# Two more pairs of token tiles with 15 block products for the channel mixer's first product, in a new order of the whole queue

## The chip, the core and the metric

The kernel runs on one core of a Trainium2 chip. The metric is device microseconds from the start to the end of one execution, and of several executions the median counts. The core has a matrix engine (PE, with its weight loads shown apart as PEld), three engines for elementwise work (DVE for vectors, ACT for activations and copies, POOL), and a queue (SP) that issues DMAs. Each engine works through its own list of instructions in program order; semaphores make one engine wait for another. Only PE writes to PSUM, from where DVE and ACT fetch the results.

## What is computed

A delta rule attention (4 batch elements, 8 heads, 768 tokens, head size 48) is followed by an MLP mixer over tokens and channels. All is in float32.

```python
for t in range(S):                      # the recurrence, for each element and head
    y[t]  = q[t] @ state
    v_old = k_n[t] @ state              # k_n: k divided by its norm
    state = state + beta[t] * outer(k_n[t], v[t] - v_old)
x = y with the heads side by side       # (4, 768, 384)
u = x + (relu(x^T @ w_tok1) @ w_tok2)^T # token mixer, 768 -> 256 -> 768
out = u + relu(u @ w_ch1) @ w_ch2       # channel mixer, 384 -> 1536 -> 384
```

## The kernel before, in words

**The recurrence** is chunked: 64 tokens a step, 12 steps an element, 48 steps in all (`recur`, job r0 to r47). Two steps make a unit of 128 tokens; there are 24 units, six an element. A unit is loaded (`load_kq`, job k), prepared (`prep`, p: norms, transposes, scaled masks), its Gram products are taken (`grams`, c and d, L440 on PE and L443 on DVE), a triangular matrix is inverted for a round of up to four units at once (`invert`, i: pairs of dependent DVE instructions L661 and L666; parts are turned by way of DRAM, L608 and L633), the halves are joined (`join`, j, L734 to L767), and v is scaled (`load_v`, v).

A step t of the recurrence goes back and forth between the engines: PE multiplies keys with the state (p_k, L790), DVE subtracts v (rest, L797), PE reads (p_y L810 and p_w L814), ACT copies (w_t, L820), PE makes the new state (p_s, L828) and the outputs (p_y, L829), DVE updates the state (s_t, L837). The next step's L790 needs that state. Element 0 has steps 0 to 11, element 1 steps 12 to 23, element 2 steps 24 to 35, element 3 steps 36 to 47.

**The mixer** of an element (`mixer`, jobs m0 to m3) can begin when its six units are written. The token mixer is L986 and L999. The channel mixer goes over three pairs of token tiles (256 tokens): transposes (L1009, copied on ACT, L1013), the first product with w_ch1, and the second product with w_ch2, which is done with 7 block products in place of 8 (L1088, whose results DVE adds to xb, L1017; the sums it needs are L1040, in `halves_of`).

For the first product there are two ways. The direct one takes 36 products of 128 x 128 with 256 columns (L1066), and ACT rectifies six results of 512 columns (L1075). In blocks of 128 tokens, 128 features and 512 channels this is 2 x 3 x 3 = 18 block products. The other way (`wide_fast`) takes 15 block products, which are 60 products of 128 x 128 with 128 columns (L958). It needs 11 sums of operands, 128 columns each (`forms`, L927 on DVE), and of its results 6 are copied by ACT (L967), 10 are added by DVE from PSUM (L970), and 6 are rectified by ACT (L974). Three PSUM buffers (tag mlp) are shared by all of the mixer.

The second way needs sums of blocks of w_ch1, too. They are made once, by job s (`sum_weights`, 16 sums, L899 and L897, on DVE), partly in place of blocks of w_ch1 that are not needed any more, partly in `lent`, the storage in which units 2, 3, 6, 7, 10 and 11 hold keys and queries. So the sums must come after the preparation of unit 11 (p11) and, where they overwrite blocks, after the direct products that read these. Before the change, all three pairs of element 0 go the direct way (`FAST = 1`) and the nine pairs of elements 1 to 3 the other.

**The order** in which all of this is emitted is one string of words, each a job's name and the number of pieces of it (a piece ends at each `yield`). Nothing else orders the work: each engine's list follows from it. It is written out in the kernel as text. Loading and rounding of weights are jobs w0 to w33 (L271 to L284; for w_ch2 L299 makes sums of blocks on DVE); x, z and Y are dummy products which keep PE busy (L225, L235).

Of the kernel before, what the change touches and what calls it, by code (L numbers as in the profile page):

```python
# [23 lines left out]
def kernel(  # L24
# [106 lines left out]
    NL = 2  # L131
# [64 lines left out]
    FAST = 1  # L196
# [145 lines left out]
    ranked = set()  # L342
    spread = set()
# [28 lines left out]
    def load_kq(u):  # L372
        b, c = divmod(u, NCH)
        kst = kst_of[slot(u)]
        if u >= TU:
            yield from load_rows(u, 0, k)
            assert last_in(u) in ranked
            yield from stacked(kst, k, u)
            yield from load_rows(u, 1, q)
            return  # L380
        for pad, src in ((kpad, k), (qpad, q)):
# [4 lines left out]
            )  # L386
            yield
            if src is k and u >= RU:
                yield from stacked(kst, k, u)

        heads = kpad[slot(u)].rearrange("t (p par) d -> t p par d", par=2)
        for cc in range(2 if u < RU else 0):
            for par in range(2):
                nc.scalar.copy(kst[PAR[par ^ cc], :, cc], heads[PAR[cc], :, par, 0:D])
                yield
# [57 lines left out]
    def prep(u):  # L453
# [7 lines left out]

        ksq = work.tile([128, NB, D], FP32, name="ksq", bufs=1)
# [20 lines left out]
        if u < TU:  # L483
            p_t = ps_turn([128, NP, 2, C], "p_t")
            for p in range(NP):
                nc.tensor.transpose(p_t[:, p], kp[:, 2 * p : 2 * p + 2], ident)
            turned.add((True, u))
# [14 lines left out]
        if u < TU:  # L502
            p_t = ps_turn([128, NP, 2, C], "p_t")
            for p in range(NP):
                nc.tensor.transpose(p_t[:, p], qp[:, 2 * p : 2 * p + 2], ident)
            turned.add((False, u))
# [220 lines left out]
    def join(u):  # L727
# [5 lines left out]
        assert done.issuperset([(u, 0), (u, 2)])  # L733
# [12 lines left out]
        for nb in range(NB):  # L746
            for r, r2 in halves:
                nc.tensor.matmul(p_z[r2, nb], wt[r, nb, HB:C], t11[r, nb])  # L748
                if before:
                    w = gm_of(before)[:, :, TC]  # L750
                    nc.tensor.matmul(p_x[r, nb], zst[r2, nb], w[r2, nb, HB:C])
        yield
        for r, r2 in halves:
# [11 lines left out]
        for nb in range(NB):  # L765
            for r, r2 in halves:
                nc.tensor.matmul(p_x[r, nb], zst[r2, nb], wt[r2, nb, HB:C])  # L767
        yield
# [96 lines left out]
    def sum_weights():  # L865
# [5 lines left out]

        a = {(j, k): (j, k) for j in range(3) for k in range(NCB)}
# [106 lines left out]
    def mixer(b):  # L979
# [42 lines left out]
        def turn_pair(c):  # L1022
# [4 lines left out]
            if b < FAST:  # L1027
# [5 lines left out]
        for c in range(0, NCH, 2):  # L1033
# [21 lines left out]
            if b >= FAST:  # L1055
# [4 lines left out]
            else:  # L1060
                for m in range(NM):
                    p_c = ps_mlp([128, 2, 2 * U], "p_c")
                    for k in range(2):
# [7 lines left out]
                        if (b, c) == (FAST - 1, NCH - 2):  # L1071
# [10 lines left out]
            turns = (*range(2, NM), 0, 1) if b >= FAST else range(NM)  # L1082
# [98 lines left out]
    r9*4 w4 i2*2 p10 i2*2 v5 i2 v5 w19 m0 r9 k10 j5 p10 i2 p10 v5 i2*2 w15 w4 v5*2  # L1181
    w4 r9*2 i2 m0 v7 k11 j5 i2 k11*2 r9 v7 j5 p10 i2 r10 v7 i2 w15*2 i2 k12 r10*3
    w15 r10 r9 m0 j5 r10*3 i2*3 r10 p10 d10 c10*3 w25 i2 c10 d10*2 w19 k12 w4 k11
    r11*3 k12*2 w19 k12 i2 r11 r10 m0 r11 i2 r11*2 d10 Y i2*3 r11 w12 r11 i2*2
    k12*3 Y w19 w21 v6 i2 v6 i2*2 m0 i2 k12 i2*2 k12*2 w12 v6 i2*2 Y v6*2 m0*2 v7
    p12*2 m0*2 c10 m0 p11*2 f6 w21 p11 f6*2 m0*2 w12*2 f7*2 m0 f7 w21 p10 m0 p11*2
    d10 w21 m0 p12 m0 j6*2 f6 p11 j6 f8*2 w25 m0 f7 f8 w23 f8 p11 j7*3 w25 p12 m0
    w25*2 r12*2 v7 r12*3 j8*2 w31 r12 t10 w23*2 t10 j8 f9*2 m0 w23 r12 r13 w23 w32
    f9 k12 r13*2 t10*2 r13 f9 p12 p11 w31*3 r12 w30 k13 p11*2 k13 m0 r13*2 d11 k13
    d11 c11*2 r13 w32*3 r13*2 d11 w30 r13 w20*2 c11 k13*2 c11*2 w30*2 r14*2 k13 d11  # L1190
    k13 d11 r14*3 p12*2 w29 m0*4 w20*2 v8 r14 k13 d12 r14 c12 d12 c12 d12 p13 c12
    d12*2 k13*2 r14 p13*2 r14*2 m0 k13*2 v8*2 r15 w23 c12*2 w25 r15*4 p12 p13*2 v8
    w33 t11 j9 m0*2 w31 r15 p13*2 t11 t12 k14*2 m0 k14 m0*2 w31 r15 m0 r15 p13
    r15*2 c13*2 w31 k14*2 d13 c13 t11 d13 c13 d13 r16 d13 r16 c13 k14 d13 w33*2 v8
    w33 w27 k14 w27 t12*3 w33 k14 t13 r16*3 w33 m0*2 j9 w27 m0*2 t11 w25 j9 r16
    t13*2 s w29 t13 w23 j9 r16*2 i3 p14 r16 w33 p14 m0 j9 v10*2 r17*2 k14 r17*2 v10
    r17 p14 v10 p14 v9 k14 p14 k15*2 i3 p14 m0*2 i3 m0 i3*3 r16 m0 i3*2 m0*2 k15
# [81 lines left out]
```

## Time and profile before

| | |
|---|---|
| median of 3 runs | 639.69 us (639.24 to 639.78) |
| profiled execution | 638.03 us |
| its span, first to last instruction | 636.3 us |
| busy PE, PEld | 606.3, 529.0 us |
| busy DVE, ACT, POOL | 447.3, 259.5, 108.7 us |
| mean granted clock of TensorE | 0.981 |
| DMA | 50.27 MB, mean 79 GB/s |

The times in the profile are of one execution. A group of instructions is one line of the kernel, with its engine, what it writes and reads, its count, its busy time and the mean length of one instruction, and then the idle time of the engine just before it and who ended it. A float32 product is two rows of PE in the trace, apart from the transposes, which are one. The ends of matmul rows are modelled, so that PE can show as busy while it waits for a short time; their starts are measured.

### The profile page before, as it was taken

What the parts mean: (1) busy time and instruction counts of PE and PEld (TensorE: products, weight loads), DVE (VectorE), ACT (ScalarE), POOL (GpSimd) and SP (SyncE); (2) the same over time, 40 slices, a digit from 0 to 9 for tenths busy, and PEclk for the clock granted to TensorE, in tenths of its full rate; (3) what the DMA queues carried; (4) which work ended last, traced back from release to release, by engine and by line L of the source; (5) the groups of instructions that cost most, each with busy time, mean ns of one, the idle gap of its engine ahead of it and who ended that gap; (6) DMA issues with size and microseconds to landing.
All of it is one profiled execution on the core that took longest, in us unless ns stands there. A gap on an engine that the chain in (4) does not pass through costs nothing.

```text
span 636.3 us, 21488 instructions
## 1 busy us (share of the span) xinstructions
PE 606.3 (95%) x9132; PEld 529.0 (83%) x9132; DVE 447.3 (70%) x1132; ACT 259.5 (41%) x631; POOL 108.7 (17%) x146
## 2 busy tenths in 40 slices
PE   8488798899999999999999999999999999999997
PEld 5367676667898988958999999769999987999997
DVE  4987876966899568988969987785627253373643
ACT  7758886447422242125623333135244230223240
POOL 2348364235301113021110010101010000000000
PEclk9878997899999999999999999999999999999999
DMA  9787568646442444354444033202020000000000
GB/s 201 131 145 170 138 133 206 151 111 155 104 111 60 92 110 92 81 131 79 92 103 101 13 94 49 66 10 38 2 54 2 27 2 0 26 1 26 1 26 26
DMA packets 135776, 50.27 MB, mean 79 GB/s; under 512 B 114656, under 2 KB 130144, under 8 KB 135680
## 3 DMA queue, kind: packets, MB, share of 16 engines
q1 hardware_dynamic: 135680, 48.89, 34.5%
q8 instruction: 72, 1.18, 0.8%
q14 instruction: 24, 0.20, 0.1%
HBM read 39.42 MB, written 9.44 MB: 77 GB/s over the span
## 4 chain that ended last, share of the span: by engine, by line
PE 81%; DVE 7%; ACT 5%; DMA 3%; issue 2%; SPq 1%; POOL 0%; DVEq 0%; ACTq 0%; POOLq 0%
PE p_o L1088 26%; PE p_r L958 19%; PE p_c L1066 7%; PE p L986 5%; PE p_h L999 5%; PE p_k L790 3%; PE p_s L828 3%; PE p_g L440 3%; PE p_y L810 3%; DMA d<-in_moe_w_ch_dram 1%; PE p_z L748 1%; PE p_ut L1009 1%; PE p_w L814 1%; DVE sub L661 1%; PE p_y L829 1%
## 5 line engine op out<-in xcount | busy, mean ns | idle before, releaser
L1088 PE MATMUL p_o<-wc,r 128*128 128x192 f32 x720 | 125.8, 329 | 0.6 <-ACT u_t L1013 0.6
L1088 PEld LDWEIGHTS p_o<-wc,r 128*128 128x128 f32 x720 | 116.7, 190 | 2.7 <-ACT u_t L1013 1.1
L970 DVE TENSOR_TENSOR r<-r,p_r 128x512 f32<-128x512 f32 x90 | 59.7, 684 | 39.9 <-PE p_r L958 38.8
L1017 DVE TENSOR_TENSOR xb<-xb,p_o 128x192 f32<-128x192 f32 x84 | 29.3, 350 | 59.5 <-PE p_o L1088 59.3
L967 ACT COPY r<-p_r 128x512 f32<-128x512 f32 x54 | 31.5, 584 | 91.4 <-PE p_r L958 89.8
L666 DVE TENSOR_TENSOR x<-x,sub 128x84 f32<-128x84 f32 (+24 forms) x178 | 59.6, 335 | 6.1
L661 DVE TENSOR_TENSOR sub<-x 128x84 f32<-128x84 f32 (+24 forms) x178 | 58.4, 328 | 7.1 <-DMA x<-n_dram 2.8
L1066 PE MATMUL p_c<-u_t,wc 128*128 128x256 f32 x216 | 51.2, 387 | 0.2 <-ACT u_t L1013 0.2
L1088 PE MATMUL p_o<-wc,s 128*128 128x192 f32 x288 | 50.5, 329 | 0.3 <-DVE xb L1017 0.3
L414 POOL TENSOR_TENSOR v_st<-v_st,nrm 128x384 f32<-128x384 f32 x24 | 20.6, 859 | 174.6 <-DMA v_st<-in_v_dram 140.7
L1088 PEld LDWEIGHTS p_o<-wc,s 128*128 128x128 f32 x288 | 46.8, 190 | 1.2 <-DVE xb L1017 0.6
L820 ACT COPY w_t<-p_w 128x192 f32<-128x192 f32 x48 | 15.3, 319 | 73.2 <-PE p_w L814 72.5
L1066 PEld LDWEIGHTS p_c<-u_t,wc 128*128 128x128 f32 x216 | 39.6, 190 | 5.9 <-ACT u_t L1013 0.4
L974 ACT ACTIVATE r<-r 128x512 f32<-128x512 f32 x54 | 33.8, 630 | 25.6 <-DVE r L970 25.3
L440 PE MATMUL p_g<-kq 48*64 48x128 f32 (+1 forms) x704 | 38.3, 290 | 3.3 <-ACT kq L509 3.3
L497 POOL TENSOR_TENSOR mb<-mask_c,cs 128x512 f32<-128x512 f32 x20 | 21.0, 1050 | 114.1 <-DVE gm L443 45.1
L842 ACT ACTIVATE xb<-p_y 64x192 f32<-64x192 f32 x96 | 31.1, 324 | 21.3 <-PE p_y L829 10.5
L958 PE MATMUL p_r<-u_t,wc 128*128 128x128 f32 x288 | 38.5, 277 | 0.0
L958 PE MATMUL p_r<-t_d,wc 128*128 128x128 f32 x288 | 37.2, 280 | 0.0
L443 DVE TENSOR_TENSOR gm<-p_g,mb 128x512 f32<-128x512 f32 x44 | 29.4, 683 | 10.0 <-PE p_g L440 7.2
L986 PE MATMUL p<-xb,w 128*128 128x384 f32 x96 | 35.6, 513 | 0.0
L958 PEld LDWEIGHTS p_r<-u_t,wc 128*128 128x128 f32 x288 | 35.3, 192 | 0.3
(177 smaller groups left out, 1200.1 us busy)
## 6 DMA issues: line engine op xcount, KB each, us to landing
d<-in_moe_w_ch_dram SPq DMA_DIRECT2D x24, 384.0 KB, 3.9
v_st<-in_v_dram SPq DMA_DIRECT2D x96, 48.0 KB, 2.5
out_dram<-xb SPq DMA_DIRECT2D x23, 192.0 KB, 1.9
kst<-in_k_dram SPq DMA_DIRECT2D x64, 48.0 KB, 3.2
n_dram<-gm SPq DMA_DIRECT2D x72, 32.0 KB, 2.4
pads<-in_k_dram SPq DMA_DIRECT2D x24, 96.0 KB, 2.4
pads<-in_q_dram SPq DMA_DIRECT2D x24, 96.0 KB, 2.5
gm<-w_dram SPq DMA_DIRECT2D x72, 32.0 KB, 2.1
```

Of the source, the lines that this page charges most:

```text
L440: nc.tensor.matmul(p_g[PAR[i ^ cc], p], kqt[f, p, cc, 0], kqt[f, p, cc])
L661: nc.vector.tensor_tensor(out=tmp, in0=y[:, :, 0:s, s : s + 1].to_broadcast([n, k, s, w]), in1=y[:, :, s : s + 1, s + 1 : m].to_broadcast( ...
L666: nc.vector.tensor_tensor(out=y[:, :, 0:s, s + 1 : m], in0=y[:, :, 0:s, s + 1 : m], in1=tmp, op=ALU.add,)
L842: nc.scalar.mul(y[:, :, D * i : D * i + D], p_y[PAR[1 - i]], 1.0 if c else -1.0)
L958: nc.tensor.matmul(p[:, i], pieces[i // width][:, at : at + 128], f[f"u{n}"], start=first and i == 0, stop=True, skip_group_check=True,)
L967: nc.scalar.copy(o, p)
L970: nc.vector.tensor_tensor(out=o, in0=o, in1=p, op=ALU.add if sign > 0 else ALU.subtract)
L974: nc.scalar.activation(o, o, ACTF.Relu)
L986: nc.tensor.matmul(p_1[dh], piece_of(w1, c, 0)[:, dh * 128 : (dh + 1) * 128], xb[:, c], start=(c == 0), stop=(c == NCH - 1),)
L999: nc.tensor.matmul(p_h, piece_of(w2, j, c * 128)[:, c * 128 : (c + 1) * 128], r1[j], start=(j == 0), stop=(j == NDH - 1),)
L1066: nc.tensor.matmul(p_c[:, k], piece_of(wc1, cb, f * 128)[:, f * 128 : (f + 1) * 128], u_t[:, cb], start=(cb == 0), stop=(cb == NCB - 1),)
L1088: nc.tensor.matmul(p, a[:, m], wc2[:, m, j], start=(start and i == 0), stop=(i == NM - 1), skip_group_check=True,)
```

## The change

Pairs two and three of element 0 (tiles 2 and 3, and 4 and 5) go the way with 15 block products; only the first pair stays direct. `FAST` is now the place (element, tile) from which on the other way holds. The weight sums so have to come between the first and the second pair of element 0. The string of the order is new from step 9 on, up to about step 36; before and after that the jobs come as they did. The rest of the diff are assertions, which build nothing (`keys_in`, `pads_in`, `held` and a loop in `sum_weights` check that an order reads nothing too early).

```diff
-    FAST = 1
+    FAST = (0, 2)
...
+        for u in range(NL, WIDE):
+            assert slot(u) < NL or u in ranked and turned.issuperset([(True, u), (False, u)])
...
-            if b < FAST:
+            if (b, c) < FAST:
                 return u_t, None
...
-            if b >= FAST:
+            if (b, c) >= FAST:
                 for ms in wide_fast(t_c, r2):
...
-                        if (b, c) == (FAST - 1, NCH - 2):
+                        if (b, c + 2) == FAST:
                             used.add(f)
...
-            turns = (*range(2, NM), 0, 1) if b >= FAST else range(NM)
+            turns = (*range(2, NM), 0, 1) if (b, c) >= FAST else range(NM)
...
-    r9*4 w4 i2*2 p10 i2*2 v5 i2 v5 w19 m0 r9 k10 j5 p10 i2 p10 v5 i2*2 w15 w4 v5*2
-    w4 r9*2 i2 m0 v7 k11 j5 i2 k11*2 r9 v7 j5 p10 i2 r10 v7 i2 w15*2 i2 k12 r10*3
+    r9*4 w4 Y r9 p10 w29 i2 w4*2 v5*4 w15 k11 i2*7 r9 i2 w15*2 i2 m0*2 x r9 j5
+    p10*2 r9*2 r10*2 k12 r10*2 v5 m0 w15 w4 i2 j5*2 i2*2 j5 r10 i2 k10 p10 i2 p10
...
-    f9 k12 r13*2 t10*2 r13 f9 p12 p11 w31*3 r12 w30 k13 p11*2 k13 m0 r13*2 d11 k13
-    d11 c11*2 r13 w32*3 r13*2 d11 w30 r13 w20*2 c11 k13*2 c11*2 w30*2 r14*2 k13 d11
+    w31 p11 w32 w31*3 p11 r13 p11 c11 k12 r13 p12 r13*2 s*4 r13 s*2 t10*3 d11 t10
+    w32*2 c11*3 s w30*4 v8*2 s c11 d11*2 w20 r14*2 d11*2 w32 p12*2 r14*3 k13*5 j9
...
```

In the changed kernel the 16 pieces of job s stand in the string between steps 13 and 16; before, twelve stood between steps 16 and 24 and four at step 28.

More of the change, by code (lines that the diff above doesn't have):

```diff
@@ L342 @@
     ranked = set()
+    keys_in = set()
+    pads_in = set()
+    held = {"t11": None, "zst": None}
     spread = set()
@@ L377, in load_kq @@
             assert last_in(u) in ranked
-            yield from stacked(kst, k, u)
+            for n, _ in enumerate(stacked(kst, k, u)):
+                if n == 3:
+                    keys_in.add(u)
+                yield
             yield from load_rows(u, 1, q)
@@ L751, in join @@
                     nc.tensor.matmul(p_x[r, nb], zst[r2, nb], w[r2, nb, HB:C])
+        assert held["zst"] == before
+        held.update(t11=None, zst=None)
         yield
+        assert held["zst"] is None
+        held["zst"] = u
         for r, r2 in halves:
```

124 lines of the change are left out of this document (65 added, 59 removed).

## Prediction

> **What bounds the kernel now.** I read the page first (busy shares, the 40 slices, the chain that ended last), then the chain in order of time, then the granted clock in short windows, and then the busy times of one stretch after another. The stretches are cut at steps of the recurrence, because the change moves everything else around these steps.
>
> ```profile
> span 636.3 us, 21488 instructions
> PE 606.3 (95%) x9132; PEld 529.0 (83%) x9132; DVE 447.3 (70%) x1132; ACT 259.5 (41%) x631; POOL 108.7 (17%) x146
> PE   8488798899999999999999999999999999999997
> DVE  4987876966899568988969987785627253373643
> PEclk9878997899999999999999999999999999999999
> ```
>
> (The last three rows are of the page's second part.) The reader is to see that PE is at 9 in nearly every slice from the ninth on, and that DVE is at 8 or 9 in many slices of the first half and only at 2 to 6 in the last third. So work taken from PE is worth its full time only where DVE can follow, and the change gives DVE work in just the half where it is nearly full.
>
> ```profile
> PE 81%; DVE 7%; ACT 5%; DMA 3%; issue 2%; SPq 1%; POOL 0%; DVEq 0%; ACTq 0%; POOLq 0%
> ```
>
> The chain confirms it: 81% of it is PE.
>
> The next rows give starts of single steps, from the timeline. "Update t" is L837 of step t (DVE), "rest t" is L797 (DVE), "read t" is the first L814 of step t (PE).
>
> ```profile
> 102.98 1.09 PE L790 MATMUL p_k<-s_t,kq 48*64 48x48 f32 x16 [0.46 <-DVE s_t L837]
> 153.07 0.35 DVE L837 TENSOR_TENSOR s_t<-s_t,p_s 128x192 f32<-128x192 f32 x1
> 214.87 0.32 DVE L797 TENSOR_TENSOR rest<-p_k,v_st 128x192 f32<-128x192 f32 x1
> 217.18 0.25 PE L814 MATMUL p_w<-rest,gm 64*64 64x48 f32 x1
> 260.38 0.43 PE L814 MATMUL p_w<-v_st,gm 64*64 64x48 f32 x8
> 402.52 0.55 PE L814 MATMUL p_w<-v_st,gm 64*64 64x48 f32 x12
> ```
>
> They are the beginning of step 9, update 13, rest 19, read 19, read 24 and read 36. Busy times of the stretches between them follow. Columns: length, then PE, PEld, DVE, ACT and POOL busy, granted clock, DMA share, GB/s.
>
> ```profile
> 103.00:153.10 50.10, 47.42 (x764) 33.73 (x766) 37.47 (x103) 25.68 (x66) 15.05 (x18) 0.93 0.63 150
> 153.10:214.90 61.80, 61.79 (x875) 55.00 (x868) 55.58 (x146) 20.20 (x52) 12.76 (x16) 1.00 0.42 98
> 214.90:217.20 2.30, 2.30 (x19) 2.08 (x17) 1.75 (x5) 0.00 (x0) 0.73 (x1) 1.00 0.50 93
> 217.20:260.40 43.20, 43.15 (x835) 37.43 (x834) 30.40 (x65) 15.35 (x41) 8.86 (x11) 1.00 0.50 106
> 260.40:402.50 142.10, 141.70 (x2203) 127.67 (x2202) 118.82 (x305) 50.89 (x122) 17.09 (x25) 1.00 0.35 79
> 402.50:636.30 233.80, 229.90 (x2557) 208.69 (x2556) 124.91 (x313) 68.05 (x142) 4.74 (x8) 1.00 0.07 19
> ```
>
> From update 13 to read 36 PE has no idle time to speak of. From update 13 to rest 19, though, DVE too is busy for 55.58 of 61.8 us: two engines are near their limits there at once.
>
> **The change, on PE.** Each of two pairs loses 36 products of 256 columns and gets 60 of 128. A product is two matmul rows in the trace. Undisturbed runs of each kind stand in the chain:
>
> ```profile
> 194.00 7.97 PE p_c L1066 x36
> 535.76 10.72 PE p_o L1088 x66
> 576.76 13.67 PE p_r L958 x120
> ```
>
> 72 rows of L1066 are 2 x 7.97 = 15.94 us; 120 rows of L958 are 13.67. A pair saves 2.27 us, both 4.5. All else on PE only moves, apart from a few dummy matmuls. The two kernels' instruction lists give the move in counts: from update 13 to read 19 the changed kernel has 33 products of L1066 less, 24 of L1088 less and one set of L958 more; from read 19 to read 24 it has 36 of L1066 less, 33 of L1088 more and the other set of L958 more; from read 24 to 36, 9 of L1088 less. At 10.72/66 = 0.162 us a row this is -14.6 - 7.8 + 13.7 = -8.7 us, then -15.9 + 10.7 + 13.7 = +8.5 us, then -2.9 us. After step 36 the two lists have the same work in the same order.
>
> The Trainium skill, "TensorE: Matmul & The Clock Gate", section "Back-to-back issue gap", has a rule against this part: with a weight load for each matmul, narrow matmuls sustain about 81 ns at 128 columns and 131 at 512, so that a column costs more the narrower the product. Worked out by its figures (an estimate, with 98 ns between them for 256) the pair would go from 72 x 98 = 7.1 to 120 x 81 = 9.7, so PE would gain work. The chain rows have 13.67 against 15.94, in float32, so I keep the measured sign.
>
> **The change, on DVE.** Both pairs now need 11 operand sums (L927) and 10 additions from PSUM (L970) each, and the 16 weight sums (L899, L897) must come before the second pair. They write into storage that the first twelve units lend, so they start only when unit 11 is prepared: in the changed list the first stands right behind update 13. Durations (busy and mean of one) are from the groups of the whole span, then from the groups of the stretch 153.1 to 214.9 alone:
>
> ```profile
> L970 DVE TENSOR_TENSOR r<-r,p_r 128x512 f32<-128x512 f32 x90 | 59.7, 684 | 39.9 <-PE p_r L958 38.8 <-ACT r L967 0.9
> L927 DVE TENSOR_TENSOR t_d<-u_t 128x128 f32<-128x128 f32 x36 | 9.5, 284 | 3.7 <-ACT u_t L1013 3.7
> L899 DVE TENSOR_TENSOR wc<-wc 128x512 f32<-128x512 f32 x7 | 5.3, 759 | 0.1
> L899 DVE TENSOR_TENSOR lent<-wc 128x512 f32<-128x512 f32 x3 | 2.2, 742 | 0.0
> L897 DVE TENSOR_SCALAR wc<-wc 128x512 f32<-128x512 f32 x1 | 0.9, 867 | 0.1
> ```
>
> ```profile
> L299 DVE TENSOR_TENSOR wc<-wc 128x192 f32<-128x192 f32 x18 | 7.4, 428 | 0.2
> L366 DVE STREAM_TRANSPOSE kq<-pads 128x512 f32<-128x512 f32 x6 | 6.6, 1106 | 0.1
> L1017 DVE TENSOR_TENSOR xb<-xb,p_o 128x192 f32<-128x192 f32 x10 | 3.5, 348 | 0.2 <-PE p_o L1088 0.2
> L1040 DVE TENSOR_TENSOR s<-s,r 128x384 f32<-128x384 f32 x4 | 2.2, 558 | 0.2
> L899 DVE TENSOR_TENSOR lent<-wc 128x512 f32<-128x512 f32 x1 | 0.7, 684 | 0.0
> ```
>
> From update 13 to rest 19 come in: 15 more weight sums at about 0.7 us, 10.5; one set of 11 operand sums at 284 ns, 3.1; 10 additions at 684 ns, 6.8; together 20.4 us. Moved out are 8 of L1040 at 0.55 (4.4), 10 of L299 at 428 ns (4.3), 3 of L1017 (1.0), a transpose L366 (1.1) and small ones (about 1.6): 12.4 us. Net +8.0 us of durations, in 8 more instructions. Neighbours overlap a little:
>
> ```profile
> 215.12 1.27 DVE L443 TENSOR_TENSOR gm<-p_g,mb 128x512 f32<-128x512 f32 x2
> ```
>
> Two of 684 ns take 1.27, so 0.1 us less for each: net +7.2, and DVE has 55.6 + 7.2 = 62.8 us of work in a stretch that took 61.8, with no wait at all. Before, it idled 6.2 us there. With none the stretch is 62.8, with as much as before 69.0. I take 2.2 of idle, 65.0 us, **+3.2**: the added sums need nothing from PE, the additions do (L970 waits 38.8 us in 90).
>
> PE can't use this time. Its queue is in program order, and read 19 waits for rest 19, and all that DVE work stands ahead of rest 19 in DVE's list; PE's own work up to there is 8.7 us less. Ahead of read 19 PE now has nothing left to do, so it follows rest 19 after 0.5 us (the 0.32 of its row and a semaphore) and not 2.3: **-1.8**. Then the delayed PE work follows, **+8.5**; DVE gets the other set of operand sums and additions there (9.9), 8 of L1040 (4.4) and about 7 of others, and loses 11 weight sums (7.6): 30.4 + 13.7 = 44.1 in 51.7, which PE covers. Then **-2.9** up to step 36.
>
> ```profile
> L967 ACT COPY r<-p_r 128x512 f32<-128x512 f32 x54 | 31.5, 584 | 91.4 <-PE p_r L958 89.8 <-issue 1.4
> L974 ACT ACTIVATE r<-r 128x512 f32<-128x512 f32 x54 | 33.8, 630 | 25.6 <-DVE r L970 25.3
> L1075 ACT ACTIVATE r<-p_c 128x512 f32<-128x512 f32 x18 | 10.7, 596 | 28.7 <-PE p_c L1066 28.6
> d<-in_moe_w_ch_dram SPq DMA_DIRECT2D x24, 384.0 KB, 3.9
> ```
>
> On ACT, 12 of L967 and 12 of L974 replace 12 of L1075, 7.4 us more in both pairs. It is idle for two thirds of the stretch (20.2 of 61.8 busy), so this costs nothing, or the length of one, 0.6 us, where PE waits for it. The DMA issues are the same 510; loads of weights move on SP's queue past the recurrence's own, and one that lands late would cost up to the 3.9 us of a transfer. I see no such wait on PE after update 13 and take nothing.
>
> **The first stretch** (step 9 to update 13). The list has 3 products of L1066 less there (-1.3) and other dummy matmuls. PE lost time in it to low clock:
>
> ```profile
> 114.00:116.00 2.00, 0.70 (x31) 0.61 (x32) 1.97 (x4) 0.00 (x0) 1.74 (x2) 1.00 0.00 0
> 116.00:118.00 2.00, 1.53 (x60) 1.40 (x53) 1.83 (x6) 1.66 (x4) 0.00 (x0) 0.81 0.94 282
> 118.00:120.00 2.00, 2.00 (x36) 1.91 (x32) 1.93 (x7) 0.69 (x3) 0.35 (x1) 0.50 1.30 186
> 120.00:122.00 2.00, 2.00 (x19) 1.09 (x20) 1.94 (x4) 0.00 (x0) 1.02 (x2) 0.84 0.92 220
> ```
>
> After 1.3 us of idle the clock is at half for (0.19 + 0.50 + 0.16) x 2 / 0.5 = 3.4 us. If that dip goes, 1.7 are won. All idle (50.1 - 47.4 = 2.7) and all low clock (0.07 x 50.1 = 3.5) gone would be -7.5 with the products; a new wait of the same kind +2. I take **-2.0**.
>
> **The sum:** -2.0 + 3.2 - 1.8 + 8.5 - 2.9 = +5.0 us. The profiled execution took 638.03 (span 636.3 and 1.7 around it), so 643.0; the median of the three runs is 639.69, and my forecast for it is **644.7**.
>
> **Rivals.**
> - *DVE is bound, but less than its durations say* and PE stays the limit everywhere: the 4.5 us of PE work and up to 1.7 of clock are won, 633.5 to 637.5. For it: DVE is idle for 12.6 us before update 13, so if update 13 comes 5 us earlier all of the above shifts. Against it: the 62.8 us, below which the changed list can't go at these durations. Decides: rest 19 no later than about 56 us after update 13, or update 13 by 147. Chance 0.20.
> - *The terms cancel*: DVE without idle (62.8) and the first stretch 5 us shorter give -5 + 1 - 1.8 + 8.5 - 2.9 = about 0: 638.4 to 641.0. Chance 0.10.
> - *Waits in both directions.* 20 additions more wait for p_r at 38.8/90 = 0.43 us each, and PE, idle for some 12 us of 65, falls to half clock once or twice (1.7 each): +4 to +8 on top, 648 to 653. It holds if DVE is idle for over 5 us between update 13 and rest 19. Chance 0.17.
> - *The change doesn't save what it says.* That it is made is certain: the lists have 36 products of L1066 and 660 of L958, before 108 and 540. But were a row of 128 columns in the first half as dear as one of L1088 (0.162), a set would take 19.4 us and not 13.7, and both +11.5: 656. Against it speaks the 13.67. Chance 0.02.
>
> The rule on narrow matmuls quoted above would bear out the last one. Beside the third stands a sentence of the Trainium skill, same page, section "What's actually happening": an idle window of about 3.4 us throttles the clock to half. The row at 114 shows that less than a whole idle window is enough here.
>
> **How the numbers follow.** My forecast has 0.51; its own range is 641.2 to 648. Faster by over 0.2% (about what a measurement of this kernel can tell from no change, 1.3 us) is the first rival: 0.20. Within 0.2%: 0.10. Slower: 0.51 + 0.17 + 0.02 = 0.70. The range leaves out the ends of the first and third rival: 636.0 to 650.5.
>
> **What would show it.** Right: read 36 about 5 us later against 402.5; update 13 to rest 19 about 65 us with DVE over 60 busy, and PE idle there by some 10 us, waiting for L797, L970 or the sums; read 19 to read 24 about 52 us; the last stretch unchanged at 233.8. Wrong: PE without idle from 150 on, or the loss sitting in the first stretch or behind step 36, where I see none.

## The result, and the profile after

The changed kernel takes 647.51 us (median of 4, 645.52 to 649.48), the kernel before, beside it, 639.74 (639.24 to 641.25). The ratio is 1.0105, its 95% interval 1.0070 to 1.0139: slower by about 1%, that is 6.7 us by the ratio and 7.8 by the two medians. Forecast were 644.7 and a range of 636.0 to 650.5. The profiled execution is the slowest of the four, 649.48 us; its stretches are read with that in mind.

The page of the changed kernel: span, engines, the granted clock in 40 slices, and the chain that ended last.

```profile
span 647.7 us, 21734 instructions
PE 611.1 (94%) x9224; PEld 537.5 (83%) x9224; DVE 461.7 (71%) x1174; ACT 266.6 (41%) x643; POOL 108.0 (17%) x146
PEclk9989897799799999999999999999999999999999
```

```profile
PE 69%; DVE 13%; DMA 5%; ACT 5%; SPq 4%; issue 3%; POOL 1%; DVEq 0%; ACTq 0%; POOLq 0%
```

The reader is to see two things. The clock row has a new 7 in the eleventh slice, where before it was at 9 from the ninth slice on. And PE's share of the chain fell from 81% to 69%; DVE's rose from 7 to 13. PE shows 4.8 us more busy time although its list became shorter in work. At half clock PE is busy for longer: by the mean clocks (0.976 of 647.7 us, 0.981 of 636.3) 3.4 us more are lost to it. The Gram products (L452, before L440), too, are busy for 43.1 us against 38.3, with 704 rows in both; why is not shown.

Busy times of the stretches between the same steps as before (columns: length, then PE, PEld, DVE, ACT and POOL busy, granted clock, DMA share, GB/s).

```profile
103.00:155.10 52.10, 48.84 (x776) 34.94 (x778) 41.23 (x114) 25.51 (x68) 16.24 (x20) 0.87 0.61 147
155.10:217.40 62.30, 58.91 (x893) 53.40 (x885) 58.79 (x153) 23.21 (x55) 13.32 (x16) 0.95 0.39 89
217.40:219.50 2.10, 2.10 (x19) 1.91 (x21) 1.96 (x8) 0.65 (x2) 0.00 (x0) 1.00 0.23 94
219.50:273.30 53.80, 52.59 (x948) 49.21 (x950) 41.48 (x99) 20.75 (x53) 8.29 (x11) 1.00 0.49 106
273.30:414.00 140.70, 139.03 (x2187) 124.97 (x2186) 116.44 (x300) 49.92 (x121) 17.60 (x26) 1.00 0.35 78
414.00:647.70 233.70, 229.82 (x2557) 208.66 (x2556) 123.62 (x308) 68.11 (x142) 4.90 (x8) 1.00 0.07 20
```

They end at update 13, rest 19, read 19, read 24, read 36 and the end. (The first row begins at a fixed time, 2 us ahead of this kernel's step 9; from step 9 to update 13 it is 49.9 us.) Against before, in us:

| stretch | forecast | before | after | difference |
|---|---|---|---|---|
| step 9 to update 13 | -2.0 | 50.1 | 49.9 | -0.2 |
| update 13 to rest 19 | +3.2 | 61.8 | 62.3 | +0.5 |
| rest 19 to read 19 | -1.8 | 2.3 | 2.1 | -0.2 |
| read 19 to read 24 | +8.5 | 43.2 | 53.8 | +10.6 |
| read 24 to read 36 | -2.9 | 142.1 | 140.7 | -1.4 |
| read 36 to the end | 0 | 233.8 | 233.7 | 0 |
| sum | +5.0 | | | +9.2 |

Step 9 itself begins 2.2 us later in this execution. That is chance: in the kernels below whose order is before's throughout, it begins between 101.5 and 107.4.

Read in pairs: from update 13 to read 19 PE had 8.7 us of work less and gained nothing; from read 19 to read 24 it got that work back in full, and 2 us more. So the question is why the stretch before rest 19 did not get shorter. PE's idle time there has few causes in the list of waits (what waited, for what, us in total, times, longest), from 155.1 to 219.5:

```profile
PE p_w L835 <- DVE rest L818: 1.8, 1, 1.8
PE p_s L849 <- ACT w_t L841: 1.6, 3, 0.6
```

The 1.8 us are read 14. (In the changed kernel L818 is before's L797, L835 is L814, L841 L820, L849 L828, L858 L837, L922 L899, L950 L927, L981 L958, L993 L970, L1040 L1017, L1111 L1088, L1063 L1040, L455 L443, L369 L366, L755 L739; in sums_one_column, order_alone and light_dve all are one higher.) The timeline of DVE shows what stands ahead of rest 14:

```profile
155.05 0.35 DVE L858 TENSOR_TENSOR s_t<-s_t,p_s 128x192 f32<-128x192 f32 x1 [0.71 <-PE p_y L850]
155.32 0.69 DVE L922 TENSOR_TENSOR lent<-wc 128x512 f32<-128x512 f32 x1
156.05 0.69 DVE L922 TENSOR_TENSOR lent<-wc,lent 128x512 f32<-128x512 f32 x1
156.66 0.69 DVE L922 TENSOR_TENSOR lent<-wc 128x512 f32<-128x512 f32 x1
...
160.39 0.69 DVE L922 TENSOR_TENSOR wc<-wc 128x512 f32<-128x512 f32 x1
161.00 1.29 DVE L455 TENSOR_TENSOR gm<-p_g,mb 128x512 f32<-128x512 f32 x2
162.19 1.08 DVE L369 STREAM_TRANSPOSE kq<-pads 128x512 f32<-128x512 f32 x1
163.13 0.34 DVE L818 TENSOR_TENSOR rest<-p_k,v_st 128x192 f32<-128x192 f32 x1
```

Rest 14 comes 8.1 us after update 13, without a gap on DVE, behind the burst of weight sums; before it came 2.0 us after it. And this is what follows on PE, in slices of 2 us:

```profile
162.00:164.00 2.00, 0.48 (x30) 0.48 (x32) 2.00 (x5) 0.00 (x0) 1.93 (x2) 1.00 0.00 0
164.00:166.00 2.00, 2.00 (x70) 1.99 (x63) 1.70 (x5) 0.34 (x2) 0.12 (x1) 0.63 0.68 161
166.00:168.00 2.00, 2.00 (x33) 1.91 (x25) 1.84 (x4) 1.05 (x3) 1.68 (x2) 0.50 0.31 62
168.00:170.00 2.00, 2.00 (x5) 1.64 (x6) 1.97 (x6) 0.51 (x2) 0.00 (x0) 0.50 0.81 228
170.00:172.00 2.00, 1.66 (x34) 0.89 (x33) 1.44 (x3) 0.83 (x2) 1.72 (x3) 0.66 0.62 98
```

(0.37 + 0.50 + 0.50 + 0.34) x 2 = 3.4 us of work lost, that is 6.8 us at half clock, behind 1.8 us of waiting. Before, the clock is at 1.00 in the whole stretch.

PE's own account of the stretch closes with these: 3.4 us of waits (1.8 for DVE, 1.6 for ACT), and 58.91 busy, of which the half clock makes about 3.3. (With the same products and the clock at 1.00, sums_one_column below has 55.60 busy.)

### The profile page after: what moved, and what is told of

Its sections match the earlier page's. It is cut to its first block, busy times and chain, and to the rows that moved or that the text cites. A ratio compares the mean times of both kernels' runs of the same rounds, so it can differ in the third digit from the quotient of the medians.

```text
span 647.7 us, 21734 instructions
## 1 busy us (share of the span) xinstructions
PE 611.1 (94%) x9224; PEld 537.5 (83%) x9224; DVE 461.7 (71%) x1174; ACT 266.6 (41%) x643; POOL 108.0 (17%) x146
## 4 chain that ended last, share of the span: by engine, by line
PE 69%; DVE 13%; DMA 5%; ACT 5%; SPq 4%; issue 3%; POOL 1%; DVEq 0%; ACTq 0%; POOLq 0%
PE p_o L1111 21%; PE p_r L981 20%; PE p_h L1022 5%; PE p L1009 5%; PE p_g L452 3%; DVE x L681 3%; DVE sub L676 3%; PE p_k L811 2%; PE p_s L849 2%; PE p_y L831 2%; PE p_c L1089 2%; DMA kst<-in_k_dram 1%; SPq L413 1%; DMA pads<-in_k_dram 1%; PE p_w L835 1%
## 5 line engine op out<-in xcount | busy, mean ns | idle before, releaser
L1111 PE MATMUL p_o<-wc,r 128*128 128x192 f32 x720 | 126.2, 329 | 0.6 <-ACT u_t L1036 0.6
L1111 PEld LDWEIGHTS p_o<-wc,r 128*128 128x128 f32 x720 | 116.7, 190 | 3.0 <-ACT u_t L1036 1.1
L993 DVE TENSOR_TENSOR r<-r,p_r 128x512 f32<-128x512 f32 x110 | 73.0, 684 | 41.9 <-PE p_r L981 38.1
L990 ACT COPY r<-p_r 128x512 f32<-128x512 f32 x66 | 38.2, 585 | 107.1 <-PE p_r L981 105.6
L1040 DVE TENSOR_TENSOR xb<-xb,p_o 128x192 f32<-128x192 f32 x84 | 29.1, 349 | 51.8 <-PE p_o L1111 51.5
L997 ACT ACTIVATE r<-r 128x512 f32<-128x512 f32 x66 | 41.3, 630 | 34.0 <-DVE r L993 33.6
L1111 PE MATMUL p_o<-wc,s 128*128 128x192 f32 x288 | 50.1, 329 | 0.5 <-DVE xb L1040 0.5
L1111 PEld LDWEIGHTS p_o<-wc,s 128*128 128x128 f32 x288 | 46.8, 190 | 1.4 <-DVE xb L1040 0.9
L981 PE MATMUL p_r<-u_t,wc 128*128 128x128 f32 x352 | 47.0, 276 | 0.0
L452 PE MATMUL p_g<-kq 48*64 48x128 f32 (+1 forms) x704 | 43.1, 292 | 3.4 <-ACT kq L524 2.8
L981 PE MATMUL p_r<-t_d,wc 128*128 128x128 f32 x352 | 45.8, 281 | 0.0
L981 PEld LDWEIGHTS p_r<-u_t,wc 128*128 128x128 f32 x352 | 43.2, 192 | 0.3
L981 PEld LDWEIGHTS p_r<-t_d,wc 128*128 128x128 f32 x352 | 41.5, 191 | 1.3 <-issue 0.2
L452 PEld LDWEIGHTS p_g<-kq 48*64 48x64 f32 (+1 forms) x704 | 32.5, 142 | 8.8 <-ACT kq L524 4.1
L284 POOL TENSOR_TENSOR wc<-w_f,d 128x384 uint32<-128x384 uint32 x24 | 25.0, 1046 | 67.2 <-DVE w_f L280 15.8
L841 ACT COPY w_t<-p_w 128x192 f32<-128x192 f32 x48 | 15.3, 318 | 47.6 <-PE p_w L835 46.8
```

Of the source, the lines that this page charges most:

```text
L452: nc.tensor.matmul(p_g[PAR[i ^ cc], p], kqt[f, p, cc, 0], kqt[f, p, cc])
L981: nc.tensor.matmul(p[:, i], pieces[i // width][:, at : at + 128], f[f"u{n}"], start=first and i == 0, stop=True, skip_group_check=True,)
L990: nc.scalar.copy(o, p)
L993: nc.vector.tensor_tensor(out=o, in0=o, in1=p, op=ALU.add if sign > 0 else ALU.subtract)
L997: nc.scalar.activation(o, o, ACTF.Relu)
L1040: nc.vector.tensor_tensor(out=xb[:, c, e], in0=xb[:, c, e], in1=p, op=ALU.add)
```

## The experiments

Three theories were to be told apart. **One:** VectorE's added work is the limit between update 13 and rest 19, as forecast. **Two:** its amount would do; it is the burst ahead of rest 14 and the half clock behind it. **Three:** the new order costs by itself, whatever the sums and products take. Each batch has its own runs of the kernel before (medians 640.57, 641.08, 639.81 and 640.81), and ratios are to these.

### Less work on VectorE

**sums_on_pool**: the weight sums go to POOL.

```diff
-                    nc.vector.tensor_tensor(out=o, in0=p, in1=q, op=op)
+                    nc.gpsimd.tensor_tensor(out=o, in0=p, in1=q, op=op)
```

> The changed kernel (647.5 us) with 15 of its 16 weight sums on POOL and not on DVE. Theory (DVE's queue between update 13 and rest 19 is the limit, 62.3 us in the profile, and PE's delayed work follows it): DVE loses about 9.4 us there, PE's own 57 us become the limit of the stretch, the time falls by 4 to 6 us, to 641.5 to 643.5, and a little less if POOL, at about 1.05 us a sum, delivers late. Rival A (the new order alone costs the time, by putting PE work behind read 19): within 1.5 us of 647.5. Rival B (the first stretch, its low clock and DMA waits, cost it): also within 1.5 us.

Measured: 656.38 us, ratio 1.0235 (1.0204 to 1.0266), slower still, and outside of what any theory had named. Its stretch from update 13 to rest 19, and the longest waits of PE and of DVE in it:

```profile
157.30:224.80 67.50, 58.14 (x893) 52.27 (x886) 55.80 (x137) 23.19 (x55) 32.23 (x32) 0.95 0.36 82
```

```profile
PE p_k L811 <- DVE s_t L858: 7.4, 2, 6.5
```

```profile
DVE s L1063 <- POOL wc L284: 5.6, 2, 4.7
```

A sum of 512 columns takes about 1.3 us on POOL against 0.69 on DVE. The rounding of the w_ch2 weights (L284) comes behind the sums on POOL, DVE's L1063 waits for it, update 14 is behind that on DVE, and PE waits 6.5 us. So this run moves the queue's jam from one engine to another and tells nothing between the theories. **w2_sums_on_pool** moves 24 other sums (L299) to POOL instead:

> The changed kernel with the 24 sums of blocks of the second product's weights (L299 of the profile before, 128x192) on POOL and not on DVE; POOL made the blocks they add up. 8 of them stand between update 13 and rest 19, 2.7 to 3.4 us. Theory 1: up to 3 us faster, 644.5 to 646.5. Theory 2: the 2 to 3 us are won only if they shorten the wait for rest 14, ahead of which none of them stands: within 1.5 us of 647.5. Either way slower if POOL's other work comes late by it.

```diff
-            nc.vector.tensor_tensor(
+            nc.gpsimd.tensor_tensor(
                 out=b[:, out], in0=b[:, x], in1=b[:, y], op=ALU.subtract
```

Measured: 648.28, ratio 1.0100 (1.0072 to 1.0127), no different from the changed kernel. The stretch is 61.8 us, and DVE is busy in it for 58.89, as much as without the edit, though with 145 instructions and not 153:

```profile
157.10:218.90 61.80, 57.49 (x891) 52.54 (x884) 58.89 (x145) 23.14 (x55) 20.19 (x24) 0.97 0.40 90
```

Fewer instructions and the same busy time: others became longer. Four of the operand sums, in the groups of L950 (duration in ns, least, median and most); in the changed kernel the same row has 283/284/291:

```profile
L950 DVE TENSOR_TENSOR t_d<-u_t x4: 281/348/911, 183.1 to 186.2; 128x128 f32<-128x128 f32 x4
```

Of the 11 operand sums in the stretch, the first three lie beside POOL's instructions and take 415, 911 and 674 ns (667 in the mean), the others 281 to 292. The eight sums that left DVE were 2.8 us of durations; the instructions that became longer give 2.5 of it back, and DVE is not relieved. This run doesn't decide either.

**sums_one_column** cuts each weight sum to its first column, so that it costs an instruction and hardly any time (the sums' other columns are left out). **no_adds** leaves out the 20 additions from PSUM of element 0.

```diff
+                o, p, q = o[:, 0:1], p is not None and p[:, 0:1], q[:, 0:1]
```

> The changed kernel with each weight sum cut to its first column, so that its place in the queue and its waits stay and only its length goes; the weights of the block products are then not the sums. Theory: as with the sums on POOL, without POOL's delay: 5 to 7 us faster than the changed kernel, 640.5 to 642.5. Rivals A and B: within 1.5 us of 647.5.

```diff
-                else:
+                elif adds:
                     nc.vector.tensor_tensor(
                         out=o, in0=o, in1=p, op=ALU.add if sign > 0 else ALU.subtract
```

> The changed kernel with the 20 additions from PSUM of element 0 left out (the copies and rectifications stay, so the first product of these pairs is incomplete). Theory: DVE loses 6 us between update 13 and rest 19 and the two-way waits with the product's three PSUM buffers: 4 to 6 us faster, 641.5 to 643.5. Rivals A and B: within 1.5 us of 647.5.

Measured: 645.02, ratio 1.0057 (1.0033 to 1.0081), and 647.26, ratio 1.0099 (1.0066 to 1.0131). The first lies between the theory's range and the rivals'; the second is no gain, as rivals A and B had it. Both cuts together, **light_dve**:

> The changed kernel with each weight sum cut to its first column and the 20 additions from PSUM of element 0 left out: the output is wrong, TensorE's work is that of the changed kernel, VectorE is relieved of both of its large additions. Theory 1: update 13 to rest 19 takes 55 to 57 us (TensorE's own 56), and the total is 639 to 642, ratio 0.997 to 1.002. Rival (the order costs by itself): no better than the cut sums alone, 644 to 646, ratio 1.005 to 1.008, with the time lost after read 19 or before update 13.

Measured: 642.56, ratio 1.0042 (1.0019 to 1.0065). The stretch from update 13 to rest 19, in sums_one_column, no_adds and light_dve:

```profile
154.10:212.00 57.90, 55.60 (x893) 50.77 (x886) 51.14 (x153) 23.11 (x55) 12.19 (x16) 1.00 0.42 96
```

```profile
151.60:212.30 60.70, 57.90 (x888) 52.63 (x880) 54.44 (x143) 23.13 (x55) 13.34 (x16) 0.94 0.41 91
```

```profile
152.40:208.70 56.30, 54.54 (x888) 49.91 (x880) 46.79 (x143) 23.01 (x55) 12.22 (x16) 1.00 0.43 99
```

Where the weight sums are cut, the stretch falls from 62.3 to 57.9 and 56.3, and the clock is at 1.00. Where only the additions are left out, DVE has 4.3 us less work, but the clock stays at 0.94, the stretch at 60.7 and the total as it was. So the weight sums matter here, and the additions hardly do. The total of light_dve stays over before's all the same, its interval begins at 1.0019; theory one alone had 639 to 642. Its loss sits behind read 19: 54.1 us to read 24.

### The place of the sums, and the clock

**sums_later** moves the first eight pieces of the weight sums behind rest 14, two by two among steps 14 and 15. **warm_14** has two dummy products (512 columns) ahead of read 14, so that PE doesn't idle there; nothing else is changed.

```diff
-    w31 p11 w32 w31*3 p11 r13 p11 c11 k12 r13 p12 r13*2 s*4 r13 s*2 t10*3 d11 t10
+    w31 p11 w32 w31*3 p11 r13 p11 c11 k12 r13 p12 r13*3 t10*3 d11 t10 w32*2 c11*3
...
+    r14 s*2 c12*3 k13 d12 r14*2 w20 r14*2 s*2 c12*2 d12*4 p13*3 p12 r15*5 s*4 m0
```

> The changed kernel with the eight pieces of the weight sums that stand between update 13 and rest 14 moved behind rest 14, two at a time, up to update 15. DVE's total between update 13 and rest 19 stays. Theory 1 (that total is the limit, as forecast): update 13 to rest 19 stays at 61 to 63 us and the time within 1.5 us of 647.5. Theory 2 (what costs is the burst: 5.5 us of sums ahead of rest 14, PE idle for 2 us behind it, and the half clock of 6.8 us that follows): read 14 comes about 3 us earlier, no low clock at 164, update 13 to rest 19 falls to 57 to 59 us and the time by 3 to 5 us, to 642.5 to 644.5. Rival A (order elsewhere): unchanged.

```diff
-    m0*5 k13*4 w20*2 r14 c12*3 k13 d12 r14*2 w20 r14*2 c12*2 d12*4 p13*3 p12 r15*5
+    m0*5 k13*4 w20*2 z*2 r14 c12*3 k13 d12 r14*2 w20 r14*2 c12*2 d12*4 p13*3 p12
```

> The changed kernel with two dummy products of 512 columns (about 1.7 us on PE) put in front of read 14, where PE waits for DVE anyway. Nothing else moves. Theory 2, its clock part: PE stays busy, the half clock of 6.8 us behind it goes, 2.5 to 3.4 us faster, 644 to 645. If the wait alone costs and not the clock, or if DVE's total is the limit (theory 1): within 1.5 us of 647.5.

Measured: 649.80, ratio 1.0131 (1.0099 to 1.0163), and 646.05, ratio 1.0074 (1.0045 to 1.0102). The stretch in sums_later, PE's three longest waits in it, and the stretch in warm_14:

```profile
151.60:214.60 63.00, 56.56 (x893) 51.01 (x884) 59.66 (x153) 23.17 (x55) 13.78 (x16) 1.00 0.39 88
```

```profile
PE p_s L849 <- ACT w_t L841: 1.6, 3, 0.6
PE p_x L767 <- DVE gm L455: 1.2, 1, 1.2
PE p_w L835 <- DVE rest L818: 1.2, 1, 1.2
```

```profile
154.40:214.30 59.90, 57.82 (x896) 51.69 (x888) 58.07 (x153) 23.28 (x55) 13.35 (x16) 1.00 0.40 93
```

In sums_later the half clock of this stretch is gone and rest 14 comes 3.4 us earlier, and the stretch is no shorter: the waits on DVE come at other places, 4.9 us in six of them. The stretch is as theory one had it, the total 2.3 us above the changed kernel's (the intervals overlap), which neither theory had. So theory two does not hold by itself. In warm_14 the clock is at 1.00 too, and the stretch is 2.4 us shorter than in the changed kernel. PE waits only for ACT in it, 2.0 us. DVE is now busy for 58.07 of 59.9 us, with 1.8 us of idle time left: with this work on DVE, nothing that helps PE can make this stretch much shorter. The clock is a part of the loss, worth about 2.4 us in this stretch (the totals, 646.05 and 647.51, have overlapping intervals). DVE's work is a floor close below, but it isn't what set the 62.3 us, as direct_new_order below shows.

**before_dve_load** turns it round: before's kernel and order, with 13 additions of 512 columns on DVE behind update 13, whose results nothing uses.

```diff
+                for _ in range(13 if t == 13 else 0):
+                    nc.vector.tensor_tensor(
+                        out=lent[:, 0:512], in0=lent[:, 512:1024],
+                        in1=lent[:, 1024:1536], op=ALU.add,
+                    )
```

> The kernel before (639.7 us) with 13 additions of 512 columns of float32, whose results nobody reads, on DVE right behind update 13: about 8 us of DVE work where the changed kernel has its sums, and no other change. Theory 1 (DVE's total between update 13 and rest 19): 55.6 + 8 = 63.6 of DVE work for 61.8 us, 2 to 6 us slower, 642 to 646. Theory 2: rest 14 comes 6 to 8 us late, PE idles for 3 to 5 us and falls to half clock: 5 to 9 us slower, 645 to 649. If DVE doesn't matter there: within 1.5 us of 639.7.

Measured: 652.25, ratio 1.0168 (1.0130 to 1.0207), 11 us, above what either theory had: the additions took DVE 10 us and not 8, and PE's wait was longer than reckoned. The stretch, and the one wait of PE in it:

```profile
156.60:228.90 72.30, 65.28 (x878) 57.63 (x871) 65.61 (x159) 20.34 (x52) 12.76 (x16) 0.95 0.36 83
```

```profile
PE p_w L814 <- DVE rest L797: 6.9, 1, 6.9
```

DVE has 10.0 us of busy time more than before (65.61 against 55.58), the stretch is 10.5 longer: 6.9 of waiting and 3.4 of half clock. A burst of DVE work at this place goes into the time in full, in before's kernel as well, although DVE is idle there for 6 us in all: its idle time comes later in the stretch, in pieces of 1.1 us at most.

### The order alone

**direct_new_order** has the new order, with direct products in all pairs of element 0 (the weight sums overwrite blocks that these read); pieces without content keep everything else in its place. **order_alone** has each weight sum cut to one column besides.

```diff
-            if (b, c) < FAST:
+            if b == 0:
+                for _ in range(6 if c else 0):
+                    yield
                 return u_t, None
...
-            if (b, c) >= FAST:
+            if b > 0:
                 for ms in wide_fast(t_c, r2):
...
                         if k == 0:
                             yield
+                            if c:
+                                yield
                     nc.scalar.activation(r2[:, m], p_c, ACTF.Relu)
                     yield
+                    for _ in range(2 if c else 0):
+                        yield
```

> The changed kernel's order with all three pairs of element 0 computed directly again (36 products of 256 columns a pair), pieces padded with empty ones so that everything else keeps its place; the weight sums keep their new place, so that the direct products read weights that are partly overwritten. DVE loses 11 operand sums and 10 additions in each of two pairs (16.7 us), PE gains 4.5. Theory: update 13 to rest 19 is then PE's, about 59 us and not 62.3, read 19 to 24 about 54, together 643 to 646. Rival A (order alone): no gain, and the 4.5 us on PE come on top, 650 to 653. Rival C (narrow products are dearer than the chain's rows): falls by more than 4.5 us, below 643, with the stretch from read 19 to 24 shorter.

> The new order with direct products in all pairs of element 0 (pieces padded so that all else keeps its place), and each weight sum cut to its first column: no narrow products, no additions, no operand sums, and next to no weight sums in element 0. The weight sums still overwrite a column of some weight blocks that the direct products read, so the output is not the reference's. TensorE has as much work as before. Theory 1 (VectorE's added work makes the loss): 640 to 643, ratio 0.999 to 1.004, update 13 to rest 19 about 57 to 59 us. Rival (the new order itself costs, with VectorE idle as well): 646 to 650, ratio 1.008 to 1.014, like the new order with full sums.

Measured: 649.89, ratio 1.0152 (1.0100 to 1.0203), and 645.84, ratio 1.0090 (1.0067 to 1.0113). The first misses the theory's 643 to 646 and comes out near rival A. Its stretch from update 13 to rest 19:

```profile
154.00:216.50 62.50, 59.76 (x839) 51.97 (x830) 53.92 (x135) 19.91 (x49) 13.30 (x16) 0.95 0.39 89
```

DVE has no operand sums and no additions there, 4.9 us less work than in the changed kernel, and is idle for 8.6 us; the stretch is as long as the changed kernel's (PE is busy for 0.85 us more). Rest 14 comes 8.1 us after update 13 again, PE waits 1.8 us for it again, and half clock follows. So it is not DVE's total that made the 62.3 us, but the burst of weight sums with the clock behind it.

The second was the surprise: here PE has as much work as before, DVE has less, and 0.9% is lost. Theory three holds for a large part. The stretches of order_alone from update 13 to read 36, and all of PE's waits in them:

```profile
154.80:212.10 57.30, 56.34 (x840) 49.29 (x832) 45.77 (x135) 19.93 (x49) 12.22 (x16) 1.00 0.42 97
212.10:215.10 3.00, 3.00 (x27) 2.71 (x26) 2.52 (x8) 0.32 (x1) 0.00 (x0) 1.00 0.48 175
215.10:270.30 55.20, 54.27 (x900) 48.27 (x902) 31.96 (x74) 17.25 (x47) 9.16 (x11) 1.00 0.46 97
270.30:410.00 139.70, 138.95 (x2187) 124.97 (x2188) 116.19 (x299) 49.96 (x121) 17.48 (x26) 1.00 0.35 79
```

```profile
PE p_s L850 <- ACT w_t L842: 2.1, 4, 0.9
PE p_w L836 <- DVE rest L819: 0.5, 1, 0.5
```

They make 255.2 us, before 249.4: 5.8 more. By before's mean durations, PE's work in them is 251.4 us against 249.7: 1.7 us stood ahead of update 13 before. (Both are estimates from counts and mean durations.) Then come 2.6 us of waits; before had 0.4, when PE had other products queued at those places. The last 1.5 us or so have no cause that is shown. The Gram products (L453 here, before L440) may hold them: PE is busy with them for 21.51 us in 412 rows, before for 18.62 in 400.

**The five parts together.** Six kernels have the new order and differ in two or three things only. In ratios to before:

| products | additions | weight sums cut | weight sums whole |
|---|---|---|---|
| direct | none | 1.0090 | 1.0152 |
| 15 blocks | none | 1.0042 | 1.0099 |
| 15 blocks | all | 1.0057 | 1.0105 |

From left to right, the length of the weight sums costs 0.62, 0.57 and 0.48%, 3 to 4 us. From the first row to the second, 15 block products with their operand sums save 0.48 and 0.53%, 3.1 to 3.4 us. From the second to the third, the additions cost 0.15 and 0.06%, 1 us or less, within the intervals. The order alone costs 0.90%, 5.8 us. 5.8 - 3.1 + 1.0 + 3.1 = 6.8 us, or 1.05% of 640; a path through the table must end at its last ratio, so this is no check of the parts. Each ratio has an interval of 0.23 to 0.5% to either side, and a difference of two some 0.3 to 0.6%. So the order's 0.90% is clear of the noise, the 0.5 to 0.6% of the sums and of the products stand at its edge and gain by coming out alike in each row or column, and the additions' cost can't be told from nothing.

### One pair, in before's order

If the order and the sums' place make the loss, a single pair might gain. **third_pair** keeps before's order, with `FAST = (0, 4)`: only the third pair goes the new way, all 16 sums are laid between the second pair's last direct product and the third pair's first, and 6 pieces with the operand sums behind its transposes. **third_pair_spread** is the same with the sums at places where DVE is idle in before's profile.

```diff
-    FAST = (0, 2)
+    FAST = (0, 4)
...
```

> Before's order of work, with the third pair of element 0 alone on 15 block products of 18. The second pair stays direct. All 16 weight sums stand between the second pair's last direct product (near rest 18) and the third pair's first product (near rest 21), where before's VectorE list has the most room; the 6 pieces with the third pair's operand sums follow its transposes, and the third pair's own pieces stand where its direct products stood. Theory 1 (what costs time is VectorE work put into a stretch that has no room for it, and the order that this forces): here the room is there, so TensorE's 2.3 us of saved work come through: 637 to 639.5, ratio 0.994 to 0.998, update 13 to rest 19 as before (about 62 us). Rival (a pair on 15 products is no gain in this part of the kernel whatever the order, since its additions wait for the products and its products for banks): 640.5 to 643, ratio 1.000 to 1.004, with the loss between read 19 and read 24.

> The kernel with the third pair alone on 15 block products, in before's order, as in third_pair, with the same VectorE work in other places: the operand sums stand behind update 18 and not ahead of it, and the 16 weight sums are laid where VectorE idles in before's profile, one or two behind the rests and updates of steps 19 to 23, the first beside step 16. In third_pair VectorE was late for update 18, rest 19 and the rests behind it by 1 to 3 us each, TensorE then idled for 0.6 to 2.6 us at a time, and four spells of half clock followed (0.88 granted between read 19 and read 24). Theory 1 (the loss comes only from where VectorE's work stands ahead of what TensorE waits for, with the clock after each wait): no such waits, full clock, 637 to 641, ratio 0.994 to 1.001, read 19 to read 24 at most 46 us. Rival (there is no room for 16 sums, 11 operand sums and 10 additions within 50 us, wherever they stand): 644 to 655, ratio 1.006 to 1.023, with waits of TensorE and half clock between read 19 and read 24 again.

Measured: 655.13, ratio 1.0228 (1.0194 to 1.0261), and 651.11, ratio 1.0158 (1.0126 to 1.0190). Both are clear misses of theory one. The rival of the second was right; that of the first had the sign, but 640.5 to 643. In third_pair 4.9 us are lost already from update 13 to rest 19 (66.7 us), the most from read 19 to read 24:

```profile
219.70:275.90 56.20, 49.13 (x882) 44.50 (x884) 37.59 (x81) 18.89 (x47) 8.46 (x11) 0.88 0.37 79
```

43.2 became 56.2 us, with 2.3 us of PE work less. (1 - 0.88) x 56.2 = 6.7 us are lost to half clock, and 7.1 to idle time; the last 1.5 us are not accounted for. In third_pair_spread the waits of PE over 1 us, from step 18 to read 24, and DVE's part in the longest:

```profile
PE p_r L981 <- DVE r L993: 3.6, 1, 3.6
PE p_w L835 <- ACT gm L755: 1.6, 1, 1.6
```

```profile
245.50 0.20 DVE L488 RECIPROCAL ksum<-ksum 128x8 f32<-128x8 f32 x1 [0.67 <-ACT ksum L485]
...
245.94 1.10 DVE L369 STREAM_TRANSPOSE kq<-pads 128x512 f32<-128x512 f32 x1
246.88 0.34 DVE L818 TENSOR_TENSOR rest<-p_k,v_st 128x192 f32<-128x192 f32 x1
247.15 0.67 DVE L922 TENSOR_TENSOR wc<-wc 128x512 f32<-128x512 f32 x1
247.74 0.68 DVE L993 TENSOR_TENSOR r<-r,p_r 128x512 f32<-128x512 f32 x1
```

The addition at 247.74 frees a buffer in PSUM (the memory that, in this kernel, PE alone writes and from which DVE and ACT fetch), and PE's next product waits for it. It stands in DVE's list behind a norm that waits for ACT, a transpose, rest 23 and a weight sum. A direct product's buffer was freed by ACT, which has room. So a pair on 15 products brings not only additions but a new dependence of PE on DVE's order, and DVE's order here was made for the other way. The 1.6 us are a link of the join's chain (L755); before, PE has no such wait between update 13 and read 36. Whether an order exists in which the third pair gains is open; two orders laid out by hand do not show that it can't.

## Why the prediction was right, and where not

The direction, the range and the place of the loss were right: after update 13, nothing behind step 36. 644.7 was 2.8 us short of the median, and the +5.0 was 4.2 short of the profiled execution's +9.2. The mechanism was right in one part (PE's work moved behind read 19) and wrong in the other (DVE's total). The three terms ahead of read 19 missed by +1.8, -2.7 and +1.6 us, which nearly cancel: that the total came out so near is in part luck. Step by step:

- **Update 13 to rest 19, +3.2.** The length came near, 62.3 us for 65.0, but not by the mechanism. The step had DVE full with 62.8 us of work and PE idle by some 10 us. DVE had 58.79: it grew by 3.2 and not by 7.2. (The 16 weight sums occupy DVE for 10.04 us there, the 11 operand sums for 2.48, the additions for 6.72; less the one sum that stood there before, the 20.4 that "come in" were 18.6, and more went out than I had counted.) PE was idle for 3.4 us, 1.8 of them for DVE. What the step put at nothing, the half clock, took about 3.3 us. And with 4.9 us less DVE work the stretch is as long (direct_new_order). So DVE lengthens it by the burst ahead of rest 14 and the clock behind it, not by its total; the total is a floor close below, which shows once the clock is mended (58.07 busy of 59.9 in warm_14) or the burst is spread (sums_later).
- **The third rival's half clock** came, with 6.8 us at half clock, but not under its condition (DVE idle for over 5 us; it was idle for 3.5). One wait of 1.8 us was enough. The forecast's own sum should have had it as a term. The range of that rival, 648 to 653, begins 0.5 us above the median.
- **Rest 19 to read 19, -1.8** failed. It assumed that PE has nothing left to do ahead of read 19. The timeline of PE in the changed kernel has products and transposes there, which end later than rest 19 at 217.4:

```profile
216.61 2.22 PE L1111 MATMUL p_o<-wc,r 128*128 128x192 f32 x12
218.66 0.82 PE L1032 MATMUL p_ut<-ident,xb 128*128 128x128 f32 x6
```

  So read 19 did not wait for rest 19 at all; DVE's burst had shown up earlier, at read 14, and as clock.
- **Read 19 to read 24, +8.5** was +10.6. The count of moved products was right (by before's durations an estimated 51.6 us of work against 42.9), but I took PE to cover all else; 1.2 us of idle time stand there that before had not, and 0.7 us have no cause that is shown. It is the same with **-2.9**, measured -1.4, with 1.3 us more idle time. These two make 3.6 of the 4.2 us by which the forecast was low. In the first of the two stretches order_alone shows it as well, 55.2 us against 43.2 with 0.9 us idle: the order by itself.
- **The first stretch, -2.0** failed: 49.9 against 50.1, and in the other kernels with the new order 47.8 to 52.9. The clock's dip at 117 did not go away; from step 9 on the stretch has a mean clock of 0.88, before 0.93. A dip of one execution was not a price to book.
- **The change on PE, -4.5** (both pairs) is -3.1 to -3.4 in the table, with the operand sums in it. So there is a saving, of the sign of the chain rows (13.67 against 15.94 us), though its size is known only to 2 us or more. The rule of the Trainium skill ("TensorE: Matmul & The Clock Gate", section "Back-to-back issue gap"), by which PE would gain work from narrow products with a weight load each, is not borne out in float32 here.
- **The first two rivals** fall by the time itself: the first wanted a gain, and even light_dve, with DVE relieved and PE's work saved, is not faster than before; the second wanted 638.4 to 641.0. The fourth, dearer narrow products, falls with the saving just named.

## What to carry to other kernels

Where an order is laid out so that one engine never waits, its work is the cover of every other engine's chain. Here the move of the work alone cost 5.8 us, more than the 4.5 us of PE work that it was made to save; price the move with the same edit made empty (order_alone), not only the instructions. Ahead of an instruction that the fullest engine waits for, a burst on another engine counts in full, even if that engine has idle time later. And a wait of near 2 us is to be booked with the half clock that may follow it: here the 1.8 us at read 14 had it behind them in all four kernels in which they stand.

## What the runs showed of the hardware

- **Short idle times throttle TensorE.** 1.8 us of waiting (1.5 idle in the 2 us shown at 162) were followed by 6.8 us at half clock, 3.4 us lost, and two dummy products in the gap removed it (warm_14). The same wait was followed by 6.8 us in direct_new_order and no_adds and by 3.4 in w2_sums_on_pool. Shorter gaps did not always do it: 1.3 us before the dip at 117 did, two waits of 1.2 us in sums_later did not. The Trainium skill, "TensorE: Matmul & The Clock Gate", section "What's actually happening", has a whole idle window of about 3.4 us as the condition; here less was enough.
- **Neighbouring sums on DVE** of 128x512 take 0.69 us each, but start 0.61 us after one another when the second doesn't read the first's result (156.05 to 156.66), and 0.73 when it does (155.32 to 156.05). On POOL the same sum takes 1.3 us (sums_on_pool).
- **DVE and POOL slow each other** when both work on two operands from SBUF: up to 911 ns against 284 for an operand sum beside POOL's instructions, and up to 1084 against a median of 598 for POOL's own sums (w2_sums_on_pool). The Trainium skill, "SBUF — State Buffer", section "Who interferes with whom", says that an instruction of DVE with two SBUF inputs contends with a POOL instruction that reads SBUF; the trace agrees.
- **One execution's start is worth little.** With the same order up to there, step 9 began between 101.5 and 107.4 us. Differences of 2 us between two single profiles say nothing ahead of that point.
